# Slots made by VectorE alone, partly ahead or inside the first set, and attention's q and k loaded half a unit sooner

## Chip, cores and metric

One core of one Trainium2 chip runs the kernel. The metric is device time in microseconds (us). TensorE is PE, VectorE DVE, ScalarE ACT, GpSimd POOL; SP is the queue that issues the transfers.

## What is computed

```python
scores = matmul(q, k.T) / sqrt(64)                 # q, k, v: 4 x 8 heads x 576 x 64
attn = matmul(scores * gamma_h ** (i - j) * (i >= j), v)
x = attn as 2304 tokens x 512
x = relu(x @ w_in) ** 2 @ w_out                    # w_in 512 x 2048
p = domain_probs / (domain_probs.sum(-1) + 1e-9)
out = sum over e < 4 of p[:, e] * (relu(x @ w1[e]) @ w2[e])   # w1[e] 512 x 1024
```

All of it is float32. Wherever a product is large, each operand is a high part (rounded to fp32r) and a low part (the rest), and a product is three matmuls: high*high, high*low, low*high.

## The kernel before

**Attention** runs over 16 units (a batch and a pair of heads). A unit n has two steps, (n, 0) with three chunks of 128 tokens and (n, 1) with the other two. In step s PE adds to a running state (`update`), makes the scores of the next step (`scores`), which DVE masks out of PSUM (`masked`: L304 for three chunks, L306 for two), then does the masked scores times v (`inner`) and the state part (`outer`). `finish` splits the result into `xh` (ACT, L375) and `xl` (DVE, L377). After step (n, 0) `prepare(n + 2)` lets POOL scale k (L272) and q (L274); after (n, 1) `load(n + 3)` puts q, k, k in its other layout (`k_n`) and v into SP's queue. The tiles of unit n + 3 take the places of unit n, so each transfer waits until PE has read these.

From step (3, 0) on, `tick(2)` after each step takes two steps of the list `work`: the conversion of the first weights, which arrive as 64-bit floats. `from_f64` makes a piece of 256 columns in seven steps: one ACT step (L102), five DVE steps (L104 to L114), and one that issues an ACT copy and two POOL subtractions (L119 to L121). The last one is followed by `load_piece` (L81), which puts the load of a further piece into SP's queue; it takes the place of the piece just converted, so it waits for DVE's L114. The step list is worked off in the program's order, and each engine and SP's queue runs its own instructions in that order.

**First MoE**: eight chunks of 256 hidden units, five groups of tokens (four of 512, one of 256). `layer1` of a job (chunk, group) runs before `layer2` of the job before it; at the start two more `layer1` go ahead. `tick(pace[0])` follows each bank that is emptied.

**Second MoE**: 16 chunks, in two passes: groups 0, 1 and 4, then groups 2 and 3. A pair of groups goes through `layer1_pair`, in which seven products of half size (Strassen's scheme in Winograd's form) replace eight. It reads seven "slots", each a half-matrix in high and low part, kept where the tokens of the first MoE were (`xh_`, `xl_`). `slots` makes them out of `yacc`, the first MoE's result: `parts` casts a half on ACT (L579) and subtracts on DVE for one column block and on POOL for the other (L580), `minus` forms differences on DVE (L587). In the first change of stage (first MoE to second) slots 4 and 5 go after the last use of group 2, slot 6 after that of group 3. In the second (first pass to second) all slots are made after the last pair of the first pass. Before that, `scale` and `rescale` bring each group to a power of two (L546 to L569).

In `layer1_pair` a bank is accumulated into twice: the product A11 goes to b1, ACT copies it (L509), then A12 is added onto it; DVE adds L503 stand between the other products in the same way. `relu_split` ends it (ACT L478, DVE L479). In the first set of each pass `tick(steps)` between the products takes steps of `work`. `split_w1` and `split_w2` cast (ACT) and subtract (POOL, both L125) the weights of the second MoE; in the second pass `drain` issues all of `split_w2` of the next chunk before the next pair.

Of the kernel before, what the change touches and what calls it, by code (L numbers as in the profile page):

```python
# [6 lines left out]
F32 = mybir.dt.float32  # L7
# [7 lines left out]
B, H, S, D = 4, 8, 576, 64  # L15
NT, DM = 2304, 512
C = 128
# [16 lines left out]
def tile_kernel(ctx, tc, qT, kT, kn, vn, v4d, mask, qdec, kdec, wd, w, probs, out):  # L34
# [179 lines left out]
    def attention(a):  # L214
# [23 lines left out]
        def load(n):  # L238
            if n >= NU:
                return  # L240
            b, a = units[n]
            q_t = ap.tile([128, S], F32, name="q_t")
            k_t = kts[n % 3]
            k_n = ap.tile([C, 4, 2, D], F32, name="k_n")
            v_n = ap.tile([C, 4, 2, D], F32, name="v_n")

            dma = nc.scalar if n == 0 else nc.sync
            nc.sync.dma_start(out=q_t, in_=qT[b, a])
            dma.dma_start(out=k_t[:, :S], in_=kT[b, a])
            if n == 0:  # L250
                dma.dma_start(out=kd, in_=kdec)
            if n < NP:
                nc.sync.dma_start(out=mk[:, a], in_=mask[:, a])
            dma.dma_start(out=k_n, in_=kn[b, a].rearrange("p (c h d) -> p c h d", c=4, h=2))
            nc.sync.dma_start(out=v_n, in_=vn[b, a].rearrange("p (c h d) -> p c h d", c=4, h=2))
            if a == 0:
                dma.dma_start(out=v4[:, b * NP : (b + 1) * NP], in_=v4d[b].rearrange("p (a h d) -> p a h d", a=NP, h=2))
            if n < NP:
                nc.sync.dma_start(out=qd[:, a], in_=qdec[:, a])
            tl[n] = (q_t, k_t, k_n, v_n)  # L260

        qs = {}

        def prepare(n):

            if n >= NU:
                return
            b, a = units[n]
            q_t, _, k_n, _ = tl[n]
            k3 = k_n.rearrange("p c h d -> p (c h) d")  # L270
            t3 = kd[:, a].rearrange("p c h -> p (c h)").unsqueeze(2).to_broadcast([C, 8, D])
            (nc.vector if n == 0 else nc.gpsimd).tensor_tensor(out=k3, in0=k3, in1=t3, op=ALU.mult)  # L272
            qs[n] = ap.tile([128, S - C], F32, name="q_s")
            nc.gpsimd.tensor_tensor(out=qs[n], in0=q_t[:, C:], in1=qd[:, a, :], op=ALU.mult)  # L274
# [5 lines left out]

        def scores(s):
            n, h = s
            q_t, k_t, _, _ = tl[n]
            qk = pq.tile([C, 2, 512], F32, name="qk")
            for c in CS[h]:
                o, m = CH[c]
                w = o - CH[CS[h][0]][0]
                for j in range(2):
                    p = slice(64 * j, 64 * j + 64)
                    nc.tensor.matmul(  # L290
                        qk[:, j, w : w + m], k_t[p, o : o + C], q_t[p, o : o + m], start=True, stop=True,
                        skip_group_check=True,
                    )
            qks[s] = qk
# [14 lines left out]
        def update(n, c):  # L309

            if n >= NU:
                return
            _, _, k_n, v_n = tl[n]
            if c == 0:
                sts[n] = pst.tile([128, D], F32, name="state")
            st = sts[n]
            for j in range(2):
                nc.tensor.matmul(  # L318
                    st[64 * j : 64 * j + 64, :], k_n[:, c, j, :], v_n[:, c, j, :],
                    start=(c == 0), stop=(c == 3), skip_group_check=True,  # L320
                )
            sb = sbs[snap_n[0] % len(sbs)]
            snap_n[0] += 1
            for j in range(2):
                p = slice(64 * j, 64 * j + 64)
                nc.scalar.copy(out=sb[p, j, :], in_=st[p, :])
            snaps[n, c + 1] = sb
# [3 lines left out]
        def inner(s, c):  # L331

            n, h = s
            v_n = tl[n][3]
            o, m = CH[c]
            w = o - CH[CS[h][0]][0]
            if c == CS[h][0]:
                xos[s] = px.tile([128, 512], F32, name="xo")
            xo, pt = xos[s], pts[s]
            for j in range(2):  # L340
                vc = v_n[:, c, j, :] if c < 4 else v4[:, n, j, :]
                nc.tensor.matmul(  # L342
                    xo[64 * j : 64 * j + 64, w : w + m], vc, pt[:m, j, w : w + m],
                    start=(w == 0), stop=(c == 0), skip_group_check=True,
                )
# [39 lines left out]
            nc.vector.memset(t[:, S:], 0.0)  # L385
        for t in sbs:
            nc.gpsimd.memset(t, 0.0)
        load(1)
        load(2)
        prepare(0)  # L390
        scores(steps[0])
        masked(steps[0])
# [3 lines left out]
        for i, s in enumerate(steps):  # L396
            n, h = s
            nxt = steps[i + 1] if i + 1 < len(steps) else None
            un, uc = (n, 2) if h == 0 else (n + 1, 0)
            update(un, uc)  # L400
            if nxt:
                scores(nxt)
                masked(nxt)
            cs = CS[h]
            for c in cs[:-1]:
                inner(s, c)
            update(un, uc + 1)
            inner(s, cs[-1])
            for c in cs:
                if c:  # L410
                    outer(s, c)
            finish(s)
            if h == 0:
                prepare(n + 2)
            else:
                load(n + 3)
            if h == 0 and n in (1, 2, 3):
                load_piece()
            if s == (3, 0):
                queue_weights()  # L420
            tick(2)

    with tc.manual_schedule():
        with ExitStack() as a:
# [55 lines left out]
                out=lo, in0=h, scalar=0.0, in1=f32(hi), op0=ALU.max, op1=ALU.subtract  # L480
            )

        def layer1_pair(c, ga, gb, steps=0):


            w1h, w1l = w1s[c]
# [18 lines left out]
            u = [tp.tile([128, GT], F32, name="r") for _ in range(2)]  # L505
            u.append(cvp.tile([128, GT], F32, name="cv_tp"))
            b1 = bank()
            product(b1, A11, 0)
            nc.scalar.copy(out=u[0], in_=b1)  # L509
            b6 = bank()  # L510
            product(b6, S2, 3)
# [59 lines left out]
                op0=ALU.mult, op1=ALU.mult,  # L571
            )

        def parts(i, src, engines=(nc.vector, nc.gpsimd)):

            for k in range(2):
                yield
                hi = slot(xh_, i)[:, k, :]
                nc.scalar.copy(out=hi, in_=src[:, k, :])  # L579
                engines[k].tensor_tensor(  # L580
                    out=slot(xl_, i)[:, k, :], in0=src[:, k, :], in1=f32(hi), op=ALU.subtract
                )

# [2 lines left out]
                yield  # L586
                nc.vector.tensor_tensor(out=o[:, k, :], in0=x[:, k, :], in1=y[:, k, :], op=ALU.subtract)  # L587

        def slots(ga, gb):


            b11, b21 = yacc[ga][:, :2, :], yacc[ga][:, 2:, :]
            b12, b22 = yacc[gb][:, :2, :], yacc[gb][:, 2:, :]

            late = (nc.vector, nc.vector)

            def first():
                yield from parts(0, b11)
                yield from minus(b11, b12, b11)
                yield from parts(1, b11)  # L600
                yield from minus(b12, b22, b12)
                yield from minus(b11, b22, b11)
                yield from parts(3, b11)
                yield from parts(2, b12)

            def second():
                yield from parts(4, b21, late)
                yield from minus(b21, b21, b11)
                yield from parts(5, b21, late)

            return first(), second(), parts(6, b22, late)

        def layer2_1(c, g):
            w2h, w2l = w2s[c]
# [73 lines left out]
        mags.update({0: place(xh_, 1, 2), 1: place(xl_, 1, 2)})  # L688
        rest = place(xh_, 7, 7)[:2] + place(xl_, 7, 7)[:2]
        scaled = {NW1 + 4: 2, NW1 + 8: 3}  # L690
        sa, sb = slots(0, 1), slots(2, 3)
        pend = []
        for i, job in enumerate(jobs):
            c, gs = job
            g = scaled.get(c)
            drain(splits[split_w1, c])

            pace[0] = 3 if c in (p, q) else 4 if c == z else 2
            if job in ((NW1, (0, 1)), (NW1 + NW2, (2, 3))):
                drain((sa if c == NW1 else sb)[2])  # L700
            if g and gs == (0, 1):
                for k in range(KT):
                    magnitude(g, k, rest[k])
            if len(gs) > 1:
                if job == (NW1 + NW2, (2, 3)):
                    held.clear()
                    queue_weights()
                layer1_pair(c, *gs, steps=3 if job == (NW1 + NW2, (2, 3)) else 0)

                if job == (NW1, (0, 1)):  # L710
                    held.difference_update({(split_w2, NW1), (split_w1, NW1 + 1)})
# [1 line left out]
            elif job == (p, (4,)):  # L713
                s = layer1(c, *gs, lambda: scale(1, mags[1]))
                rescale(1, s)
                work.insert(0, sa[0])
            else:
                layer1(c, *gs)
            if i == last[c]:
# [1 line left out]
            if job == (p, (3,)):  # L721
                s = scale(0, mags[0])
            if job == (q, (2,)):
                work.insert(0, sa[1])
            if job == (q, (3,)):
                work.insert(0, sa[2])
            if job == (z, (0, 1)):
                drain(splits[split_w2, z])
                work[:0] = sb
            if g and gs == (4,):  # L730
                rescale(g, s)
            pend.append((i, job))

            while i > 1 and len(pend) > 1:
                j, done = pend.pop(0)
                drain(splits[split_w2, done[0]])
                layer2(done)
                if j == last[done[0]]:
                    queue_weights((split_w2, done[0] + 2))
                    if c >= NW1 + NW2:  # L740
                        drain(splits.get((split_w2, done[0] + 2)))
            if job == (p, (3,)):
                rescale(0, s)
# [67 lines left out]
```

## Time and profile before

| what | value |
|---|---|
| median of three runs | 1256.74 us (1250.98 to 1257.46) |
| the profiled execution | 1251.88 us, its span 1250.1 us |
| PE busy | 1223.1 us, 98% |
| DVE, POOL, ACT busy | 840.6 us, 526.2 us, 452.4 us |
| granted TensorE clock | full speed in every slice |

Busy times are sums over the whole span. A matmul of 512 columns counts as busy for 390 ns, though 48 of them in a row take 10.88 us, so PE's idle time is a little less than the time lost between matmuls.

### The profile page before, as it was taken

The page shows a single profiled execution, that of the slowest core. Times are in us where ns is not written, and L with a number is a line of the kernel's source. Part 1 is how long each engine was busy: PE and PEld are TensorE (multiplying, and loading weights), DVE is VectorE, ACT ScalarE, POOL GpSimd, SP SyncE. Part 2 cuts the span into 40 slices and gives each one's busy share as a digit, 9 for nine tenths or more (in the row PEclk, how much of TensorE's full clock was granted, in tenths as well). Part 3 has the DMA queues.
Part 4 walks back from the last instruction along what each step waited for, and adds up shares of the span by engine and source line. Part 5 has one row for each costly group of instructions (what it writes and reads, how often), then busy time and mean ns, then how long its engine had stood idle before and what let it go on. Part 6 is the DMA issues. An engine that isn't in the chain of part 4 may idle for free.

```text
span 1250.1 us, 17901 instructions
## 1 busy us (share of the span) xinstructions
PE 1223.1 (98%) x6576; PEld 1027.6 (82%) x6576; DVE 840.6 (67%) x1406; ACT 452.4 (36%) x1109; POOL 526.2 (42%) x635
## 2 busy tenths in 40 slices
PE   7989999999999998999999999999999999999998
PEld 6778888888888886888888888888778888888887
DVE  3775677787877687356756666565865676767665
ACT  3545433333333334533323323232335333333330
POOL 4555545555555445443422334222354343434340
PEclk9999999999999999999999999999999999999999
DMA  9741111111111000111111111110041111111111
GB/s 336 255 143 43 43 49 45 47 47 43 51 44 51 26 1 18 55 59 40 43 42 35 34 51 42 43 35 34 20 150 42 60 50 52 51 51 51 51 43 67
DMA packets 41303, 76.31 MB, mean 61 GB/s; under 512 B 4864, under 2 KB 5888, under 8 KB 41216
## 3 DMA queue, kind: packets, MB, share of 16 engines
q1 hardware_dynamic: 40704, 74.47, 17.5%
q8 instruction: 51, 0.84, 0.3%
q10 hardware_dynamic: 512, 0.70, 0.2%
q14 instruction: 36, 0.29, 0.1%
HBM read 70.44 MB, written 4.72 MB: 60 GB/s over the span
## 4 chain that ended last, share of the span: by engine, by line
PE 90%; DVE 5%; ACT 2%; DMA 1%; issue 1%; POOL 1%; ACTq 0%; POOLq 0%; DVEq 0%; SPq 0%
PE o L653 30%; PE h L496 24%; PE h L462 18%; PE o L621 14%; PE xo L342 1%; DVE xl L580 1%; PE qk L290 1%; DMA k_n<-kn 1%; PE xo L354 1%; DVE y L587 1%; PE state L318 1%; DVE y L553 1%; DVE r L467 1%; ACT xh L579 1%; DVE y L629 0%
## 5 line engine op out<-in xcount | busy, mean ns | idle before, releaser
L653 PE MATMUL o<-w2hi,ghi 128*128 128x512 f32 x576 | 224.8, 390 | 2.7 <-DVE oacc L661 2.7
L661 DVE SCALAR_TENSOR_TENSOR oacc<-o,pr,oacc 128x512 f32<-128x512 f32 x270 | 197.1, 745 | 42.5 <-PE o L653 41.9
L653 PE MATMUL o<-w2hi,glo 128*128 128x512 f32 x576 | 224.3, 389 | 0.0
L653 PE MATMUL o<-w2lo,ghi 128*128 128x512 f32 x576 | 224.1, 389 | 0.0
L125 POOL TENSOR_TENSOR w2lo<-wraw,w2hi 128x256 fp32r<-128x256 f32 x128 | 94.3, 764 | 206.3 <-ACT w2hi L124 206.3
L496 PE MATMUL h<-xh,w1hi 128*128 128x512 f32 x448 | 174.8, 390 | 4.9 <-ACT r L509 3.8
L496 PE MATMUL h<-xl,w1hi 128*128 128x512 f32 x448 | 174.4, 389 | 0.0
L496 PE MATMUL h<-xh,w1lo 128*128 128x512 f32 x448 | 174.3, 389 | 0.0
L125 POOL TENSOR_TENSOR glo<-r,ghi 128x512 fp32r<-128x512 f32 (+1 forms) x80 | 96.5, 1207 | 148.0 <-ACT ghi L124 147.1
L462 PE MATMUL h<-xh,w1hi 128*128 128x512 f32 (+1 forms) x448 | 154.1, 344 | 1.3 <-DVE xl L377 1.3
L462 PE MATMUL h<-xl,w1hi 128*128 128x512 f32 (+1 forms) x448 | 154.0, 344 | 0.0
L462 PE MATMUL h<-xh,w1lo 128*128 128x512 f32 (+1 forms) x448 | 153.9, 344 | 0.0
L125 POOL TENSOR_TENSOR w1lo<-wraw,w1hi 128x256 fp32r<-128x256 f32 x112 | 89.3, 797 | 131.9 <-ACT w1hi L124 131.9
L503 DVE TENSOR_TENSOR r<-h,r 128x512 f32<-128x512 f32 x96 | 66.4, 691 | 95.5 <-PE h L496 89.4
L653 PEld LDWEIGHTS o<-w2hi,ghi 128*128 128x128 f32 x576 | 108.2, 188 | 26.0 <-DVE oacc L661 4.0
L653 PEld LDWEIGHTS o<-w2lo,ghi 128*128 128x128 f32 x576 | 108.1, 188 | 22.6
L653 PEld LDWEIGHTS o<-w2hi,glo 128*128 128x128 f32 x576 | 108.2, 188 | 21.7
L621 PE MATMUL o<-glo,w2hi 128*128 128x512 f32 (+1 forms) x320 | 118.1, 369 | 1.6 <-POOL glo L125 1.6
L621 PE MATMUL o<-ghi,w2hi 128*128 128x512 f32 (+1 forms) x320 | 117.9, 369 | 0.3 <-ACT ghi L124 0.3
L621 PE MATMUL o<-ghi,w2lo 128*128 128x512 f32 (+1 forms) x320 | 117.7, 368 | 0.0
L467 DVE TENSOR_TENSOR r<-r 128x512 f32<-128x512 f32 (+1 forms) x80 | 63.8, 798 | 69.8 <-ACT r L466 69.6
L496 PEld LDWEIGHTS h<-xh,w1hi 128*128 128x128 f32 x448 | 84.1, 188 | 24.0 <-ACT r L509 4.6
(97 smaller groups left out, 2090.4 us busy)
## 6 DMA issues: line engine op xcount, KB each, us to landing
wraw<-w SPq DMA_DIRECT2D x128, 256.0 KB, 2.7
wraw<-wd SPq DMA_DIRECT2D x64, 256.0 KB, 2.7
q_t<-qT SPq DMA_DIRECT2D x16, 288.0 KB, 4.4
out<-oacc SPq DMA_DIRECT2D x18, 256.0 KB, 2.0
kt<-kT SPq DMA_DIRECT2D x15, 288.0 KB, 5.0
v_n<-vn SPq DMA_DIRECT2D x16, 256.0 KB, 4.7
k_n<-kn SPq DMA_DIRECT2D x15, 256.0 KB, 5.0
qd<-qdec SPq DMA_DIRECT2D x4, 224.0 KB, 5.2
```

The costliest lines, as they stand in the source:

```text
L125: nc.gpsimd.tensor_tensor(out=lo, in0=src, in1=f32(hi), op=ALU.subtract)
L290: nc.tensor.matmul(qk[:, j, w : w + m], k_t[p, o : o + C], q_t[p, o : o + m], start=True, stop=True, skip_group_check=True,)
L318: nc.tensor.matmul(st[64 * j : 64 * j + 64, :], k_n[:, c, j, :], v_n[:, c, j, :], start=(c == 0), stop=(c == 3), skip_group_check=True,)
L342: nc.tensor.matmul(xo[64 * j : 64 * j + 64, w : w + m], vc, pt[:m, j, w : w + m], start=(w == 0), stop=(c == 0), skip_group_check=True,)
L354: nc.tensor.matmul(xo[64 * j : 64 * j + 64, w : w + m], sb[:, j, :], qs[n][:, o - C : o - C + m], start=False, stop=True, skip_group_check ...
L462: nc.tensor.matmul(h, wk(a, f, k), x[:, k, :], start=(n == 0), stop=(n == 3 * KT - 1))
L467: nc.vector.tensor_tensor(out=r, in0=r, in1=r, op=ALU.mult)
L496: nc.tensor.matmul(o, a[:, i, k, :], slot(x, j)[:, k, :], start=(first and n == 0), stop=(n == 5), skip_group_check=True,)
L503: v.tensor_tensor(out=o, in0=x, in1=y, op=ALU.add)
L621: nc.tensor.matmul(o, a[:, f, 128 * m : 128 * m + 128], x[:, f, :], start=(n == 0), stop=(n == 3 * FT - 1))
L653: nc.tensor.matmul(o, a[:, f, 128 * m : 128 * m + 128], x[:, f, :], start=(n == 0), stop=(n == 3 * FT - 1))
L661: nc.vector.scalar_tensor_tensor(out=acc, in0=o, scalar=pr[:, tt, e : e + 1], in1=acc, op0=ALU.mult, op1=ALU.add)
```

## The change

Attention: `load(n + 3)` without v comes after step (n, 0), right behind `prepare(n + 2)`; v follows after step (n, 1), by a function of its own. `tick` takes one step after (n, 0) and two after (n, 1).

Start of the first MoE: four `layer1` go ahead of the first `layer2` (three before), and `work` takes four steps at a time in the first three jobs.

Slots: every subtraction is on DVE. `slots` has a fourth part, `ahead`, with the cast of A11 and four of the differences. In the first change of stage it runs where the first part ran, and slot 6 is made inside the first set, by its ticks. In the second, A11 goes to slot 7, which no pair reads in the first pass, and `ahead` is put at the end of `work` half a pass earlier; the pairs of the second pass read slot 7.

Second pass: the weights of chunk 25's second layer are no longer issued before chunk 25's pair.

```diff
@@ attention
-            dma.dma_start(out=k_n, ...)
-            nc.sync.dma_start(out=v_n, in_=vn[b, a]...)
+            dma.dma_start(out=k_n, ...)
+            if n == 0:
+                load_v(n)
...
+        def load_v(n):
+            if n < NU:
+                b, a = units[n]
+                vs[n] = ap.tile([C, 4, 2, D], F32, name="v_n")
+                nc.sync.dma_start(out=vs[n], in_=vn[b, a].rearrange("p (c h d) -> p c h d", c=4, h=2))
...
-        load(1)
-        load(2)
+        for n in (1, 2):
+            load(n)
+            load_v(n)
...
             if h == 0:
                 prepare(n + 2)
+                load(n + 3)
             else:
-                load(n + 3)
+                load_v(n + 3)
...
-            tick(2)
+            tick(1 + h)
@@ second MoE
-        def layer1_pair(c, ga, gb, steps=0):
+        def layer1_pair(c, ga, gb, steps=0, s0=0):
...
-            product(b1, A11, 0)
+            product(b1, A11, s0)
...
-                engines[k].tensor_tensor(
+                nc.vector.tensor_tensor(
                     out=slot(xl_, i)[:, k, :], in0=src[:, k, :], in1=f32(hi), op=ALU.subtract
                 )
...
-        def slots(ga, gb):
+        def slots(ga, gb, s0=0):
...
+            def ahead():
+                yield from parts(s0, b11)
+                yield from minus(b11, b12, b11)
+                yield from minus(b12, b22, b12)
 
             def first():
-                yield from parts(0, b11)
-                yield from minus(b11, b12, b11)
                 yield from parts(1, b11)
-                yield from minus(b12, b22, b12)
                 yield from minus(b11, b22, b11)
                 yield from parts(3, b11)
                 yield from parts(2, b12)
...
-            return first(), second(), parts(6, b22, late)
+            return ahead(), first(), second(), parts(6, b22)
@@ the jobs
-        sa, sb = slots(0, 1), slots(2, 3)
+        sa, sb = slots(0, 1), slots(2, 3, 7)
...
-            pace[0] = 3 if c in (p, q) else 4 if c == z else 2
-            if job in ((NW1, (0, 1)), (NW1 + NW2, (2, 3))):
-                drain((sa if c == NW1 else sb)[2])
+            pace[0] = 4 if i < 3 else 3 if c in (p, q) else 4 if c == z else 2
+            if job == (NW1, (0, 1)):
+                drain(sa[2])
+                work.insert(0, sa[3])
+            if job == (NW1 + NW2, (2, 3)):
+                drain(sb[3])
...
-                layer1_pair(c, *gs, steps=3 if job == (NW1 + NW2, (2, 3)) else 0)
+                steps = 3 if job == (NW1 + NW2, (2, 3)) else 2 if job == (NW1, (0, 1)) else 0
+                layer1_pair(c, *gs, steps, 7 if c >= NW1 + NW2 else 0)
...
-                work.insert(0, sa[0])
+                work[:0] = sa[:2]
...
             if job == (q, (2,)):
-                work.insert(0, sa[1])
-            if job == (q, (3,)):
                 work.insert(0, sa[2])
             if job == (z, (0, 1)):
                 drain(splits[split_w2, z])
-                work[:0] = sb
+                work[:0] = sb[1:]
             if g and gs == (4,):
                 rescale(g, s)
+                if g == 3:
+                    work.append(sb[0])
...
-            while i > 1 and len(pend) > 1:
+            while i > 2 and len(pend) > 1:
...
-                    if c >= NW1 + NW2:
+                    if c >= NW1 + NW2 and done[0] != z:
                         drain(splits.get((split_w2, done[0] + 2)))
```

## Rows read from the trace of the kernel before

**Rows 1.** Stretches: PE, weight loads, DVE, ACT, POOL busy (instructions); clock, DMA share, GB/s.
```profile
438.17:497.72 59.55, 54.31 (x283) 44.98 (x282) 49.81 (x71) 24.98 (x52) 30.76 (x28) 1.00 0.03 9
497.72:894.41 396.69, 396.69 (x1928) 335.88 (x1927) 245.34 (x389) 132.18 (x316) 140.96 (x189) 1.00 0.12 42
894.41:938.95 44.54, 39.77 (x183) 31.77 (x181) 32.72 (x52) 16.85 (x41) 19.77 (x24) 1.00 0.31 107
```

**Rows 2.** Chain of waits, whole span: start, us, what; two stretches of matmuls.
```profile
104.32 10.88 PE o L621 x48
126.08 2.87 PE h L462 x24
```

**Rows 3.** Chain of waits in attention.
```profile
14.13 0.99 PE qk L290 x12
...
46.95 0.87 PE qk L290 x12
...
51.29 0.87 PE qk L290 x12
...
54.77 5.20 DMA k_n<-kn
...
81.15 0.87 PE qk L290 x12
...
86.62 0.73 DVE cv_b L114
```

**Rows 4.** PE's waits from 14 to 88 us: total, times, longest.
```profile
PE xo L342 <- DVE pt L304: 3.5, 4, 1.3
PE h L462 <- DVE xl L377: 1.3, 1, 1.3
PE state L318 <- POOL k_n L272: 1.2, 1, 1.2
```

**Rows 5.** SP's queue in order of time.
```profile
53.40 0.33 SPq L81 DMA_DIRECT2D wraw<-wd  x1
53.83 0.37 SPq L248 DMA_DIRECT2D q_t<-qT  x1
```

**Rows 6.** SP's waits, 0 to 90 us: total, times, longest.
```profile
SPq L81 <- DVE cv_b L114: 33.1, 7, 8.3
...
SPq L248 <- PE qk L290: 5.2, 6, 1.6
```

**Rows 7.** DVE in order of time, in attention.
```profile
43.24 1.24 DVE L114 SCALAR_TENSOR_TENSOR cv_b<-wraw,cv_tp 128x256 f32<-128x256 uint32 x1
...
52.21 1.12 DVE L114 SCALAR_TENSOR_TENSOR cv_b<-wraw,cv_tp 128x256 f32<-128x256 uint32 x1
...
58.96 0.42 DVE L114 SCALAR_TENSOR_TENSOR cv_b<-wraw,cv_tp 128x256 f32<-128x256 uint32 x1
```

**Rows 8.** POOL in order of time, in attention.
```profile
43.02 1.18 POOL L274 TENSOR_TENSOR q_s<-q_t,qd 128x448 f32<-128x448 f32 x1
```

**Rows 9.** PE's waits from 438 to 498 us.
```profile
PE h L496 <- ACT r L509: 1.8, 1, 1.8
PE o L621 <- POOL glo L125: 1.6, 3, 0.7
PE h L496 <- DVE cv_tp L503: 1.2, 1, 1.2
```

**Rows 10.** Slot subtractions, 438 to 498 us: ns min/median/max, first and last start.
```profile
L580 DVE TENSOR_TENSOR xl<-y,xh x10: 674/748/1777, 454.5 to 490.9; 128x512 fp32r<-128x512 f32 x10
...
L580 POOL TENSOR_TENSOR xl<-y,xh x4: 1297/1345/1737, 455.0 to 466.2; 128x512 fp32r<-128x512 f32 x4
```

**Rows 11.** PE's waits from 880 to 940 us.
```profile
PE o L653 <- DVE oacc L661: 2.7, 3, 1.6
PE h L496 <- ACT r L509: 2.0, 1, 2.0
```

**Rows 12.** Chain of waits at the second change of stage.
```profile
929.20 2.86 DMA wraw<-w
```

More of the change, by code (lines that the diff above doesn't have):

```diff
@@ L244, in load @@
             k_n = ap.tile([C, 4, 2, D], F32, name="k_n")
-            v_n = ap.tile([C, 4, 2, D], F32, name="v_n")
             dma = nc.scalar if n == 0 else nc.sync
@@ L254, in load @@
             dma.dma_start(out=k_n, in_=kn[b, a].rearrange("p (c h d) -> p c h d", c=4, h=2))
-            nc.sync.dma_start(out=v_n, in_=vn[b, a].rearrange("p (c h d) -> p c h d", c=4, h=2))
+            if n == 0:
+                load_v(n)
             if a == 0:
@@ L259, in load @@
                 nc.sync.dma_start(out=qd[:, a], in_=qdec[:, a])
-            tl[n] = (q_t, k_t, k_n, v_n)
-        qs = {}
+            tl[n] = (q_t, k_t, k_n)
+        vs, qs = {}, {}
+        def load_v(n):
[3 more added lines that the diff above has]
+                nc.sync.dma_start(out=vs[n], in_=vn[b, a].rearrange("p (c h d) -> p c h d", c=4, h=2))
         def prepare(n):
@@ L268, in prepare @@
             b, a = units[n]
-            q_t, _, k_n, _ = tl[n]
+            q_t, _, k_n = tl[n]
             k3 = k_n.rearrange("p c h d -> p (c h) d")
@@ L282, in scores @@
             n, h = s
-            q_t, k_t, _, _ = tl[n]
+            q_t, k_t, _ = tl[n]
             qk = pq.tile([C, 2, 512], F32, name="qk")
@@ L312, in update @@
                 return
-            _, _, k_n, v_n = tl[n]
+            k_n, v_n = tl[n][2], vs[n]
             if c == 0:
@@ L333, in inner @@
             n, h = s
-            v_n = tl[n][3]
+            v_n = vs[n]
             o, m = CH[c]
@@ L572, in rescale, with parts @@
             )
-        def parts(i, src, engines=(nc.vector, nc.gpsimd)):
+        def parts(i, src):
             for k in range(2):
@@ L587, in minus @@
                 nc.vector.tensor_tensor(out=o[:, k, :], in0=x[:, k, :], in1=y[:, k, :], op=ALU.subtract)
-        def slots(ga, gb):
+        def slots(ga, gb, s0=0):
             b11, b21 = yacc[ga][:, :2, :], yacc[ga][:, 2:, :]
             b12, b22 = yacc[gb][:, :2, :], yacc[gb][:, 2:, :]
-            late = (nc.vector, nc.vector)
+            def ahead():
+                yield from parts(s0, b11)
+                yield from minus(b11, b12, b11)
+                yield from minus(b12, b22, b12)
             def first():
-                yield from parts(0, b11)
-                yield from minus(b11, b12, b11)
                 yield from parts(1, b11)
-                yield from minus(b12, b22, b12)
                 yield from minus(b11, b22, b11)
@@ L606, in second @@
             def second():
-                yield from parts(4, b21, late)
+                yield from parts(4, b21)
                 yield from minus(b21, b21, b11)
-                yield from parts(5, b21, late)
-            return first(), second(), parts(6, b22, late)
+                yield from parts(5, b21)
+            return ahead(), first(), second(), parts(6, b22)
         def layer2_1(c, g):
```

## Prediction

> **What bounds the kernel.** I read the busy table first: PE is busy 98% of the span at the full clock (2.4 GHz throughout), so a change that removes no matmul can win back only PE's gaps. In the busy time by stretch the long stretch of the first pass shows PE busy for all of its 396.69 us, and so does the first MoE until its last jobs; the gaps lie in three places, two of them in [rows 1]. I size each by its count of matmuls: 48 of 512 columns take 10.88 us, 0.227 each, and 24 of 256 take 2.87, 0.120 each [rows 2].
>
> - Attention. Unit 8 begins at 46.95 and unit 9 at 51.29: an undisturbed unit takes 4.34 us. From 14.13 to 81.15 there are 14 units, 67.0 us, where 14 x 4.34 = 60.8: 6.3 lost [rows 3]. A further 1.3 is waited at the end [rows 4].
> - First change of stage, 59.55 us long [rows 1]. By the program it holds 170 matmuls of 512 columns, 96 of 256 and 16 of one column (about 0.1): 38.6 + 11.5 + 1.6 = 51.7. Lost: 7.8.
> - Second change of stage, 44.54 us [rows 1]: 156 and 24 matmuls, 35.4 + 2.9 = 38.3. Lost: 6.3.
>
> Together 21.7 us, the most that the change could give.
>
> **Attention, part by part.** PE's waits show three causes: 3.5 us in four waits for the masking L304, 1.2 for the scaled `k_n`, 1.3 at the end for `xl` [rows 4]; what the count has beyond these (6.3 - 3.5 - 1.2 = 1.6) is waits too short for that view.
>
> *The `k_n` wait.* SP issued a weight piece (L81) at 53.40 and q of unit 11 only at 53.83 [rows 5]; the `k_n` behind it landed at 54.77 + 5.20 = 59.97 [rows 3], and POOL and PE waited. The piece had waited for DVE's L114, 1.12 us long at 52.21 [rows 7]. These holds sum to 33.1 us, the longest 8.3 [rows 6]. Counting the steps (seven a piece, three a unit from unit 3), pieces are now issued after steps (5, 1), (7, 1), (10, 0), (12, 1) and (14, 1). The only one that follows a step (n, 0) now stands behind that load's q and k instead of before it; the others stand behind v, and their L114 runs at the latest early in the next unit, while SP's next q waits for PE's scores in its middle. So no piece holds up a load, and I take the 1.2 as gained (bounds 0 and 1.3).
>
> *The L304 waits.* Between `finish(n, 0)` and the large masking DVE had two conversion steps, now one. Some steps last far longer than others: L114 0.42 us at 58.96 but 1.12 and 1.24 at 52.21 and 43.24 [rows 7], the last while POOL makes q_s (43.02, for 1.18) [rows 8]. At 52.21 the slot held one DVE step: it ended 2.04 us after unit 9's start, and no wait over 0.15 us followed [rows 3, 4, 7]. So about 2.1 us after the unit's start is the limit, and one step at its worst length so far (1.24, from 0.92 after the start: 2.16) costs 0.1. By the count of steps 9 of the 13 slots hold a DVE step, so 0.9 stays, and I leave 0.3 for ACT's part. Of 5.1 (3.5 + 1.6) 3.9 is gained. Bounds: 5.1 if no step meets POOL; at the other end each step waits out a whole q_s and then takes its own 0.42: 0.92 + 1.18 + 0.42 = 2.52 after the start, 0.45 late, nine times 4.0.
>
> *The end.* L114 stood before the last `xl` for 0.73 us [rows 3]; the slot after (15, 0) now holds ACT's step. I take 0.4 (bounds 0 and 0.7).
>
> Attention: 1.2 + 3.9 + 0.4 = 5.5 gained.
>
> *What is put off.* 26 steps of two become 13 units of three: 13 of 52 conversion steps move behind attention, and 17 of chunk 0's second layer are open. The first three jobs take 3 x 2 x 4 = 24 steps, and that layer is needed only after four `layer1` of 24 matmuls, 21.8 us. Even one piece after the other, a piece in the worst 2 us of its DVE rows [rows 7] plus its ACT and POOL parts, 2.5 pieces fit. I cost this at nothing; without that cover it would be at most some 5 us.
>
> **First change of stage, 7.8 lost.** PE waits 1.6 for POOL's glo, 1.8 for ACT's copy L509, 1.2 for the add L503 [rows 9]; the rest is shorter waits, and some 1.0 for `scale`, which is left alone.
>
> Four subtractions move from POOL to DVE here. On POOL one takes 1.35 us, on DVE 0.67 at best, but up to 1.78 where both engines work at once [rows 10]. DVE thus does four more at 0.67, 2.7 us, and is spared about as much blocking: three others stretched by up to 1.1 each. The count of DVE's time to the last slot of `first` comes out within some 0.3; what follows starts some 1.5 us sooner, since the pair of blocked instructions at its end goes. That removes the shorter wait at `layer2` of the small group, 1.4. POOL's own queue, eight weight splits ahead of glo, shifts by as much as PE, so of the 1.6 I take 0.45. Slot 6 (two casts, two subtractions) no longer stands before L509 and L503: L509 comes about 2 us sooner, but PE arrives 1.9 sooner too, so 0.45; L503's 1.2 goes, but the two subtractions now stand before the add that the last product needs, and of it 0.9 comes back: 0.4 with the short waits there. Sum 1.4 + 0.45 + 0.45 + 0.4 = 2.7. Bounds: 6.8 gained, all except `scale`; or 1.3 lost, if the four subtractions at 1.78 each put some 4 us more on DVE.
>
> The Trainium skill's page "SBUF — State Buffer", section "Who interferes with whom", says that a DVE instruction with two SBUF inputs and a POOL instruction that reads SBUF cannot run together, and the later one waits for the whole of the earlier; 1.78 against 0.67, a difference near POOL's duration, agrees. [...]
>
> **Second change, 6.3 lost.** PE waits 2.7 for DVE's accumulation L661, whose banks DVE empties late because the slots stand before it; by the count of matmuls 3.7. DVE had 18 slot instructions there, now 16, and POOL four, now none; one of DVE's waited 1.2 for POOL in turn. 16 x 0.62 and the L661 between put the eighth L661 some 3 us sooner; 0.6 of 3.7 stays, 3.1 gained (bounds 1.5 and 3.7). PE waits 2.0 (2.3 by the count) for L509 [rows 11]: ACT was to cast weights that landed only after a transfer begun at 929.20, 2.86 long [rows 12]. Those four casts now come in the next `layer2`. Its 16 ticks then hold exactly the casts (5 steps) and the next first layer (11), so the transfer before the pair of chunk 26 starts late as well, by my count about 1 us after that pair instead of 2: 0.65 comes back there. Gained 1.7 (bounds 0 and 2.3). Sum 4.8. `ahead` runs in the first pass, where DVE is busy 245.3 of 396.7 us [rows 1]: nothing.
>
> **Sum.** 5.5 + 2.7 + 4.8 = 13.0 us. The profiled execution took 1251.88, 1.8 more than its span; that gives 1238.9. The other runs lie at 1250.98, 1256.74 and 1257.46; the median, 1256.74, is 4.9 above the profiled one. From the mean of the four, 1254.3, the forecast is 1241.3, and I predict 1241.
>
> **Rivals.**
> 1. *The early load does nothing.* SP waits for PE's scores before q [rows 6] in either order, so only the held piece matters, and `k_n` could stay late by another one: the 1.2 is not gained. 1242.5. Against it: the order above.
> 2. *POOL keeps blocking the one step.* Nine slots at 0.45 leave 4.0 instead of 0.9: gain 9.9, 1244.4. For it: two of three L114 shown are blocked [rows 7, 8].
> 3. *DVE is the limit at both changes of stage.* Seven subtractions at 0.6 come on top and no blocking goes: 4.2 less, gain 8.8, 1245.5. For it: DVE is busy 49.8 of 59.6 us at the first [rows 1]. Against: 1.78 [rows 10].
> 4. *Both 2 and 3, and the late cast moves whole to chunk 26:* gain 13.0 - 3.1 - 4.2 - 1.7 = 4.0, 1250.3: no change that can be told.
> 5. *Slower: the pieces hold the loads.* Each of five pieces stands before q and k of some unit. A `k_n` has about 3.5 us to spare (two units to its use, less its landing at 5.20 and POOL). Five holds like the longest, 8.3 [rows 6], cost 5 x 4.8 = 24: 11 more than the gain, 1265. It decides from a hold of 3.5 + 13/5 = 6.1. Against: each L114 has run by then.
>
> **Chances.** Forecast 0.5, rivals in order 0.1, 0.13, 0.12, 0.1, 0.05. Less than about 0.5% (6.3 us) cannot be told from no change here. Faster is the forecast and rivals 1 to 3: 0.85; same 0.10; slower 0.05. Range 1233 to 1250: below, the gain near its bound (18 from 1251); above, rival 4. The forecast's own is 1236 to 1246.
>
> **What would show it.** Right: units of 4.34 us nearly all through, L304 waits under 1.5, no `k_n` wait, the first MoE beginning near 82; no POOL L580, short L580 on DVE; the first set still waiting for L509, the second pass's wait at chunk 25 gone and a small one at 26. Wrong: L304 late with one step, waits inside the first set over 3 us, or a gap at the first `layer2`.

## Result and profile after

The changed kernel takes 1239.65 us (median of 4 runs, 1238.53 to 1240.66); the kernel before took 1254.37 on the same chip (4 runs, 1250.98 to 1257.46). The ratio is 0.9887, 95% interval 0.9868 to 0.9906. The profiled execution took 1239.68 with a span of 1237.9: 12.2 us less than before, where the sum of the prediction was 13.0. In the changed file the lines have moved: the scores are L296, the masking L310, the state copy L332, `xl` L383; a set's adds are L512 and its copy L518; glo is awaited by `layer2` L630, the accumulation is L670, a slot's subtraction L589.

First the changed kernel's stretches of the two changes of stage, in the columns of [rows 1], between the same events.

```profile
433.62:490.51 56.89, 53.97 (x283) 44.93 (x282) 48.61 (x75) 25.14 (x52) 25.21 (x24) 1.00 0.03 10
...
887.20:926.50 39.30, 39.22 (x184) 32.36 (x183) 29.08 (x49) 14.30 (x34) 15.09 (x18) 1.00 0.31 108
```

The first is 2.66 us shorter than in [rows 1], the second 5.24. DVE's column is the one to read: in the first it does 75 instructions in 48.61 us, where it did 71 in 49.81. It has four more subtractions and is busy 1.2 us less.

PE's waits in the changed kernel, from 13 to 90, 425 to 500 and 870 to 950 us, in the columns of [rows 4].

```profile
PE h L471 <- DVE xl L383: 0.8, 1, 0.8
PE xo L348 <- DVE pt L310: 0.2, 1, 0.2
...
PE o L630 <- POOL glo L125: 1.0, 2, 0.7
PE h L505 <- ACT r L518: 0.7, 1, 0.7
PE h L505 <- DVE cv_tp L512: 0.7, 1, 0.7
PE po L569 <- DVE r L557: 0.3, 1, 0.3
...
PE h L505 <- ACT r L518: 0.3, 1, 0.3
```

Attention: L310 falls from 3.5 to 0.2, the `k_n` wait is gone and the last one falls from 1.3 to 0.8 [rows 4]. First change of stage: glo 1.6 to 1.0 (one of its three waits, 0.56, was the small group's), the copy 1.8 to 0.7, the add 1.2 to 0.7, the last at another product than before [rows 9]. Second: the accumulation's 2.7 is gone and the copy's 2.0 is 0.3 [rows 11].

What is left in attention is seen in the chain of waits of the changed kernel, in one slot, and in POOL's row at that time.

```profile
41.15 0.49 ACT xh L381
41.66 0.56 DVE xl L383
42.22 1.05 DVE cv_tp L104
43.27 0.88 DVE pt L310
44.19 0.66 PE xo L348 x8
```

```profile
41.98 1.14 POOL L280 TENSOR_TENSOR q_s<-q_t,qd 128x448 f32<-128x448 f32 x1
```

The one conversion step that is left (L104, which takes 0.28 us at best) ends at 43.27, 0.15 after POOL's q_s, and the masking, the `xo` product and the rest follow it. By the matmuls' starts the masking is late in four units, by 0.1 to 0.25 us.

### The profile page after: what moved, and what is told of

The parts are those of the page before. It is cut to its first block, busy times and chain, and to the rows that moved or that the text cites. A ratio compares the mean times of both kernels' runs of the same rounds, so it can differ in the third digit from the quotient of the medians.

```text
span 1237.9 us, 17902 instructions
## 1 busy us (share of the span) xinstructions
PE 1221.7 (99%) x6576; PEld 1027.7 (83%) x6576; DVE 843.7 (68%) x1414; ACT 451.0 (36%) x1109; POOL 517.9 (42%) x627
## 4 chain that ended last, share of the span: by engine, by line
PE 92%; DVE 4%; ACT 2%; DMA 1%; issue 1%; POOL 0%; ACTq 0%; DVEq 0%
PE o L662 30%; PE h L505 24%; PE h L471 18%; PE o L630 15%; PE xo L348 2%; PE qk L296 1%; DVE xl L589 1%; PE xo L360 1%; PE state L324 1%; DVE y L596 1%; DMA k_n<-kn 0%; DVE r L476 0%; DVE y L638 0%; DVE y L562 0%; ACT xh L588 0%
## 5 line engine op out<-in xcount | busy, mean ns | idle before, releaser
L670 DVE SCALAR_TENSOR_TENSOR oacc<-o,pr,oacc 128x512 f32<-128x512 f32 x270 | 196.9, 745 | 41.2 <-PE o L662 40.7
L512 DVE TENSOR_TENSOR r<-h,r 128x512 f32<-128x512 f32 x96 | 66.4, 691 | 86.7 <-PE h L505 77.4
L630 PE MATMUL o<-glo,w2hi 128*128 128x512 f32 (+1 forms) x320 | 118.1, 369 | 1.0 <-POOL glo L125 1.0
L630 PE MATMUL o<-ghi,w2hi 128*128 128x512 f32 (+1 forms) x320 | 117.8, 368 | 0.0
L630 PE MATMUL o<-ghi,w2lo 128*128 128x512 f32 (+1 forms) x320 | 117.7, 368 | 0.0
```

Of the source, the lines that this page charges most:

```text
L512: v.tensor_tensor(out=o, in0=x, in1=y, op=ALU.add)
L630: nc.tensor.matmul(o, a[:, f, 128 * m : 128 * m + 128], x[:, f, :], start=(n == 0), stop=(n == 3 * FT - 1))
L670: nc.vector.scalar_tensor_tensor(out=acc, in0=o, scalar=pr[:, tt, e : e + 1], in1=acc, op0=ALU.mult, op1=ALU.add)
```

## Experiments

A time without a range is a single execution. Places are compared in the profiled executions. A matmul's lateness is the distance to the next matmul's start less the 0.227 or 0.120 us of [rows 2].

In attention I compare from the scores of unit 2 to the second scores of unit 15. Unit 1 starts with its score matmuls 0.21 us apart in some executions and 0.11 in others, of the same kernel, which moves all of attention by up to 1 us. Undisturbed that distance is 13 x 4.34 + 2.28 = 58.7.

**The two halves alone.** One kernel has the attention of after and the slots of before, the other the reverse.

> The attention part alone (q and k loaded sooner, three conversion steps a unit, four first-layer jobs ahead), slots as before. Theory (three places that add up): the first MoE begins 4.5 us sooner, as in the changed kernel, and the two changes of stage lose what they lost before (7.8 and 6.3): about 4.5 us faster than before. Rival (what attention wins is given back, because the 13 conversion steps that were put off and the fourth early job crowd the first MoE): a gap of some us at the first second-layer job or at chunk 1, and under 2 us gained in the span.

> The slot part alone (subtractions on VectorE, slot 6 in the first set, the part ahead, chunk 25's casts later), attention and the first jobs as before. Theory: attention ends near 87.5 us as before, the first change of stage loses 5.1 instead of 7.8 and the second 1.3 instead of 6.3: 7.7 us faster. Rival (part of this gain came only because attention ended sooner): less than 6 us.

Attention alone: 1248.04 (ratio 0.9943, 0.9926 to 0.996). Unit 2 to 15 takes 59.8 where before took 64.8 and after 60.2. The first change of stage takes 59.55 us (432.38 to 491.93), exactly as before, and the waits are those of before, here from 870 to 950 us:

```profile
PE o L662 <- DVE oacc L670: 2.7, 3, 1.6
PE h L505 <- ACT r L518: 2.1, 1, 2.1
```

Slots alone: 1245.89 (0.9921, 0.9899 to 0.9943). Its first change of stage takes 56.87 us (441.19 to 498.06), where after takes 56.89. Its attention waits at the same places as before (from 13 to 92 us):

```profile
PE xo L342 <- DVE pt L304: 4.1, 4, 1.5
PE h L462 <- DVE xl L377: 1.3, 1, 1.3
PE state L318 <- POOL k_n L272: 1.1, 1, 1.1
```

Unit 2 to 15 takes 66.8 in this execution, 1.9 more than in before, part of it a stretch at half clock (last section); two executions of the same attention differed by that much here. The halves touch different places, and at the first change of stage neither disturbs the other. In the medians they gain 7.8 and 9.9 us, where 4.5 and 7.7 were expected: together more than the 14.7 of the whole. But the kernel before has a median of 1255.79 beside the halves and of 1254.37 beside the whole, and its executions range from 1250.98 to 1258.27, so this sum decides nothing.

**The halves of the attention change.** First the early load with two steps in every slot, then one step after (n, 0) with the load where it was.

```diff
@@ early load, two steps
-            tick(1 + h)
+            tick(2)
@@ late load, fewer steps
             if h == 0:
                 prepare(n + 2)
-                load(n + 3)
             else:
+                load(n + 3)
                 load_v(n + 3)
```

> The changed kernel, but two conversion steps after every step of attention again; the loads stay early. Theory (steps and loads cure different waits): the masking waits of 3.5 us come back, the wait for the scaled k stays away because the weight piece now stands behind q and k in the queue; 14 units take 65.5 us instead of 62.3. Rival (the early load does nothing by itself): the wait of 1.2 us for the scaled k comes back as well, 14 units take 67 us as before.

> The changed kernel, but q, k and v of unit n + 3 all loaded after step (n, 1) as before; one and two conversion steps stay. Theory: SP waits for TensorE's reads in either order, and with this count of steps no weight piece that has to wait stands in front of q and k (the only one after a step (n, 0) follows VectorE's step of the unit before): 14 units take 62.3 us as in the changed kernel, so the early load is worth nothing once the steps are fewer. Rival (the early load is what keeps k in time): a wait for the scaled k of 1 us or more, 14 units take 63.5 us or more.

Early load with two steps: 1243.80; unit 2 to 15 takes 63.6, 1.2 less than before. The `k_n` wait is gone and the masking's is nearly whole (13 to 92 us):

```profile
PE xo L348 <- DVE pt L310: 3.0, 4, 0.9
PE h L471 <- DVE xl L383: 1.3, 1, 1.3
PE state L324 <- ACT st L332: 0.2, 1, 0.2
```

Late load with fewer steps: 1239.99; unit 2 to 15 takes 60.0, as in after, and there is no `k_n` wait either:

```profile
PE h L471 <- DVE xl L383: 0.8, 1, 0.8
PE xo L348 <- DVE pt L310: 0.2, 1, 0.2
```

So each half removes the `k_n` wait by itself, and only the fewer steps remove the rest. With them the early load is worth nothing that shows (at most some 0.3). SP's queue shows how each half does it. In before the piece ahead of the late `k_n` was held for 4.8 us, from behind this transfer until 53.40 [rows 5], with q, k and `k_n` behind it:

```profile
48.23 0.33 SPq L255 DMA_DIRECT2D v_n<-vn  x1
```

With the early load and two steps these three are issued ahead of that piece, as the prediction has it (`k_n` at 51.72, the piece at 54.33). With the late load and fewer steps the piece still stands ahead of them, but is held for 2.3 us only (issued at 50.23).

**Where the step stands.** None after (n, 0), three after (n, 1): no conversion step is left ahead of the large masking.

```diff
-            tick(1 + h)
+            tick(3 * h)
```

> The changed kernel, but all three conversion steps of a unit come after step (n, 1) and none after (n, 0). Theory (what is left in attention is the one step that stands before the large masking while GpSimd scales q; before the small masking there is about 1 us to spare, and a step takes 0.3 to 0.4 where nothing blocks it): 14 units take 61.0 to 61.3 us instead of 61.8 to 62.7. Rival (three steps in a row make the small masking late): 62.5 us or more, with waits for the small masking.

1241.27; unit 2 to 15 takes 60.8, 0.6 more than after, where about 1 us less was expected. The masking L310 is never late, so the cause was right, but another wait came, seen in its waits from 13 to 90 us and in its chain from 39.84 on:

```profile
PE state L324 <- ACT st L332: 1.3, 2, 0.7
PE h L471 <- DVE xl L383: 0.8, 1, 0.8
PE xo L348 <- DVE pt L312: 0.2, 1, 0.2
```

```profile
39.84 0.34 DVE cv_b L114
...
40.20 0.02 ACT cv_tp L102
...
40.55 0.20 ACT st L332
...
40.76 0.22 ACT st L332
...
41.02 0.34 PE state L324 x4
```

With three steps in a row one slot can hold a piece's last DVE step (L114) and the next piece's first ACT step (L102). ACT then waits in L102 for DVE, and the state copies L332 that PE needs stand behind it. It happens at 40 and at 71 us, 0.9 and 0.8 late by the matmuls' starts. The end of attention, outside the distance compared, takes 0.4 longer than in after as well: there the small masking L312 is late, as the rival had it, though by far less.

**POOL's subtractions back** for slots 0 to 3, one column block each, with all else as in after (slots 4 to 6 were on DVE alone in the kernel before too):

```diff
-                nc.vector.tensor_tensor(
+                (nc.gpsimd if k and i < 4 else nc.vector).tensor_tensor(
```

> The changed kernel, but the subtractions of the second column block of slots 0, 1, 2 and 3 are on GpSimd again (four at the first change of stage, three at the second); all else is as changed. Theory (GpSimd's subtractions cost VectorE in blocking as much as they spare it, and the blocked pair at the end of the first part is what the small group's second layer waited for): the first change of stage loses 6.3 us instead of 5.1, with the wait at the small group back at 1.2 to 1.4; the second loses 2 to 2.5 instead of 1.3. Rival (VectorE is simply the limit there): with seven subtractions of 0.6 us taken off it the two places lose less than in the changed kernel, 3 us in all instead of 6.4.

1240.76. Waits from 425 to 500 (the first two rows of it) and 870 to 950 us:

```profile
PE o L630 <- POOL glo L125: 1.6, 3, 0.7
PE h L505 <- ACT r L518: 0.8, 1, 0.8
...
PE o L662 <- DVE oacc L670: 0.7, 1, 0.7
```

The gaps of the small group's second layer are back, 1.3 us (0.48 at 461.95 and 0.83 at 462.55), as in before (0.51 and 0.82). PE's waits name glo, but POOL's queue is not the cause: in before POOL has ended its two subtractions 0.80 us ahead of glo and waits for ACT's cast of `ghi`, and this cast waits for DVE's square L467, held to 1.51 us beside them (0.41 in after). DVE's row, then two of POOL's:

```profile
466.73 1.51 DVE L467 TENSOR_TENSOR r<-r 128x256 f32<-128x256 f32 x1
...
464.96 2.99 POOL L580 TENSOR_TENSOR xl<-y,xh 128x512 fp32r<-128x512 f32 x2
468.75 0.86 POOL L125 TENSOR_TENSOR glo<-r,ghi 128x256 fp32r<-128x256 f32 x1 [0.80 <-ACT ghi L124]
```

With POOL's subtractions back the rows repeat: the square takes 1.50, and glo starts 0.80 after POOL's pair. So it is the blocked pair on DVE, as expected. The stretch of the first change takes 58.05 us, 1.16 more than in after, and DVE is busy longer with four instructions fewer (columns of [rows 1]):

```profile
432.00:490.05 58.05, 54.22 (x283) 45.00 (x282) 49.27 (x71) 25.13 (x52) 30.84 (x28) 1.00 0.03 10
```

In the second change the accumulation is late by 0.83 instead of 0.24: 0.6, less than expected. The total hides both, as this execution's attention ended 1.6 us sooner.

**Slot 6 ahead of the first set**, as the kernel before had it:

```diff
-                drain(sa[2])
-                work.insert(0, sa[3])
+                drain(sa[3])
...
-                steps = 3 if job == (NW1 + NW2, (2, 3)) else 2 if job == (NW1, (0, 1)) else 0
+                steps = 3 if job == (NW1 + NW2, (2, 3)) else 0
...
+            if job == (q, (3,)):
+                work.insert(0, sa[3])
```

> The changed kernel, but slot 6 is made before the first set of the second MoE again, by VectorE, as before. Theory: the two casts and two subtractions stand before the copy and the adds again: the wait for the copy grows from 0.9 to 1.8 us, the wait for the second add (about 1.2) is back, and the 0.9 before the last product goes: the set loses 3.2 us instead of 2.1. Rival (it makes no difference where they stand, they only move the wait within the set): 2.1 us in the set, within 0.3.

1240.45. The copy is 1.95 late again (0.91 in after) and the 0.9 before the last product is gone; the add's wait does not come back. The copy's row, 425 to 500 us:

```profile
PE h L505 <- ACT r L518: 1.8, 1, 1.8
```

From 484.6 to 488 PE ran at a granted clock of 0.55, so it reached the add later; what the add would have cost at full clock is not seen. Slot 6 inside the set thus wins the copy's 1.0 and puts a wait of 0.9 at the last product; what it wins in all is not shown.

**Fewer weight splits ahead of glo**: around the small group and in group 2's first layer a tick takes one step of `work` instead of three, and three again after it.

```diff
+            if job == (q, (2,)):
+                pace[0] = 1
...
+            if job in ((q, (4,)), (q, (2,))):
+                pace[0] = 1 if job == (q, (4,)) else 3
```

> The changed kernel, but the first weights of the second MoE are worked off more slowly while the small group's second layer of chunk 6 and the first layer of group 2 of chunk 7 are issued (one step of the list at a time instead of three), so that three of the eight weight splits stand in GpSimd's queue before that group's low part instead of eight. Theory (the 1.6 us wait at that group's second layer is GpSimd's queue): the wait falls to 0.3 or less, and the first change of stage loses 4 us instead of 5.1. Rival (the low part is late because the square is late on VectorE): the wait stays over 1 us.

1238.40. Its waits from 425 to 500 us:

```profile
PE h L505 <- ACT r L518: 1.5, 1, 1.5
PE po L569 <- DVE r L557: 0.4, 1, 0.4
PE h L505 <- DVE cv_tp L512: 0.3, 1, 0.3
```

Glo's 1.3 at group 2's second layer is gone, so the splits ahead of it were the cause. But PE now comes sooner to the first set, and the copy's lateness grows from 0.91 to 1.67; the last product's falls from 0.90 to 0.43. Net 1.0 by these places; the stretch (433.34 to 488.90) is 1.3 shorter, as the matmul behind each longer wait is some 0.1 late too.

**The early issue of chunk 25's weights put back**, a single execution first and then more of them:

```diff
-                    if c >= NW1 + NW2 and done[0] != z:
+                    if c >= NW1 + NW2:
```

> The changed kernel, but the weights of chunk 25's second layer are issued before its pair again. Theory: the wait of 2 us for the copy of the first product comes back at chunk 25's pair and the one of 0.5 us at chunk 26's pair goes; the second change of stage loses 2.9 instead of 1.3, or a little less where the transfer starts sooner now. Rival (the transfer begins sooner because the slots are done sooner, so the wait would have gone by itself): no wait over 0.7 us at chunk 25's pair.

> The changed kernel with chunk 25's second-layer weights issued before its pair again, now timed, to see in how many executions the wait of 2 us is followed by a drop of the granted clock. Theory (the wait brings the drop on): a mean granted clock under 1.000 in most executions, and 1241 to 1243.5 us: 1.6 of wait and up to 1.8 of half clock over the changed kernel. Rival (the drop in the one profile was chance): 1.000 in most executions and 1241.2 us.

1243.42, then 1242.67 (1242.11 to 1243.71) against 1239.80 for after on the same chip. The copy waits again, 2.2 us and 2.6 us late at chunk 25, and nothing at chunk 26. What follows the wait costs as well. The first of the two kernels in three stretches, columns as in [rows 1], the clock third from the end:

```profile
920.00:923.00 3.00, 1.24 (x6) 0.70 (x4) 0.00 (x0) 0.96 (x3) 2.55 (x5) 1.00 0.91 275
924.20:927.50 3.30, 3.30 (x9) 2.58 (x8) 1.24 (x2) 0.60 (x1) 0.00 (x0) 0.51 0.32 112
927.80:930.00 2.20, 2.20 (x11) 1.81 (x10) 1.37 (x3) 0.63 (x1) 0.00 (x0) 1.00 0.00 0
```

PE is idle for more than half of the first, and in the second its clock is 0.51 of full speed, the lower of its two levels (1.2 GHz): 9 matmuls in 3.3 us, where the third has 11 in 2.2.

**All together**: fewer splits ahead of glo, `tick(3 * h)`, POOL for slot 6's subtractions, and no early issue of any next chunk's weights in the second pass; beside it after itself on the same chip.

```diff
-            tick(1 + h)
+            tick(3 * h)
...
-            return ahead(), first(), second(), parts(6, b22)
+            return ahead(), first(), second(), parts(6, b22, e6)
...
-        sa, sb = slots(0, 1), slots(2, 3, 7)
+        sa, sb = slots(0, 1, 0, nc.gpsimd), slots(2, 3, 7)
...
-                    if c >= NW1 + NW2 and done[0] != z:
-                        drain(splits.get((split_w2, done[0] + 2)))
```

> The changed kernel with four edits together: all three conversion steps after step (n, 1); fewer weight splits ahead of the low part of group 2; slot 6's subtractions on GpSimd within the first set, where it has nothing else to do; and no early issue of second-layer weights before any pair of the second pass. Theory (each takes one remaining wait: 1 us in attention, 1.6 at group 2's second layer of which 0.8 comes back at the copy of the first product, 0.4 to 0.9 before the last product of the set, 0.6 at chunk 26): 2.5 to 3.5 us less than the changed kernel on the same chip, about 1237. Rival (the waits move to the next place that VectorE's backlog reaches, the copy of the first product above all): within 1 us of the changed kernel.

> The changed kernel once more, beside the version with four edits and the kernel before on one chip. Theory (the kernel before has waits of about 2 us after which the granted clock of TensorE drops for some microseconds in part of its executions; the changed kernel has none that long): a mean granted clock of 1.000 in nearly all executions of the changed kernel and 0.996 to 0.998 in most of the kernel before, which puts the measured gain some 2 us over the 12.2 us that the two profiles show. Rival (the clock has nothing to do with the waits): the same share of executions under 1.000 in both.

1238.85 (1238.71 to 1238.98; ratio to before 0.9878, 0.9861 to 0.9895) against 1239.80 (1238.53 to 1241.27; 0.9884, 0.9865 to 0.9902). The ranges overlap: no difference that can be told, where 2.5 to 3.5 us were expected; the rival's bound of 1 us held. Its waits at the late places are two, 425 to 500 us, and none from 870 to 950:

```profile
PE h L505 <- ACT r L518: 1.5, 1, 1.5
PE po L569 <- DVE r L557: 0.3, 1, 0.3
```

Glo, the last product and chunk 26 are mended, and the copy takes back half: the first change of stage takes 55.04 us (435.19 to 490.24), 1.85 less than in after. But `tick(3 * h)`, which was expected to gain 1 us, costs 1.1 to 1.5 from unit 2 to the first MoE (65.1, where the two profiled executions of after take 64.0 and 63.6). Without that edit it should come out some 1 us lower; that was not run.

## Why the prediction came out

**Attention.** Forecast 5.5 gained, measured 5.1 from unit 2 on: 4.6 in the units (64.8 to 60.2) and 0.5 at the end (1.3 to 0.8; forecast 0.4). The first MoE begins 4.5 us sooner, at 83.16 for 87.67, because unit 2 began 0.6 later in this execution. 1.5 us are still lost in the units, where the forecast left 1.2. By the matmuls' starts the masking has 0.7 of it (forecast 0.9) and ACT's state copies 0.55 (0.30 and 0.25 in two units; forecast 0.3). The size was right, its division was not: the 1.2 of the `k_n` wait was put down to the early load, and the fewer steps alone remove it too. So the first rival is right that beside the fewer steps the early load does nothing, yet not in its price, since nothing was lost by it.

The Trainium skill's page "SBUF — State Buffer", section "Who interferes with whom", names `tensor_scalar` among the operations that can take the port pair that DVE shares with POOL. The row of L104 at 42.22, 1.05 for 0.28 beside POOL's q_s, agrees; the prediction had used the rule for two SBUF inputs alone.

**What was put off.** No wait stands at the first jobs of the MoE after `xl`'s, so the cover was there.

**First change of stage.** 2.7 forecast, 2.66 measured, out of terms that missed by about the same in both directions; that the sum came out so close is luck:

| term | forecast | measured (lateness before, after) |
|---|---|---|
| small group's second layer | 1.4 | 1.2 (1.33, 0.14) |
| glo at group 2 | 0.45 | 0 (1.32, 1.32) |
| the copy in the first set | 0.45 | 1.0 (1.91, 0.91) |
| adds in the first set | 0.4 | 0.4 (1.31, 0.90) |

The first term came by the mechanism that was forecast, the blocked pair on DVE. The second was sized on the 1.6 of [rows 9], of which 0.56 was the small group's. At group 2 POOL's splits stand ahead of glo as before and moved with PE. That delay at glo gives ACT's copy time, and the copy's term came out larger for it. The run with fewer splits shows the exchange: 1.3 gone at glo, 0.8 more at the copy. The two terms were in large part one: how early PE reaches the set. The add's return by 0.9 at the last product came as forecast.

**Second change.** 4.8 forecast. The stretch is 5.24 shorter, and 0.5 comes back at chunk 26, outside it: 4.7. The accumulation is late by 0.24 where it was late by 3.2 (0.45, 1.81 and 0.97); the casts of chunk 25 had 2.19 and have nothing, chunk 26 has 0.5 (forecast 0.65). Of the accumulation's 3.0, the largest term, 0.6 comes back with POOL's subtractions; the rest is put down to the slot parts made in the first pass, as the forecast counted, but no run took these back alone, so it is not shown. Issuing the casts later is worth 1.7 by the places, and with them put back the median is 2.9 us higher, half clock after the wait included.

**DVE as the limit**, the third rival, fell by the run with POOL's subtractions back: with four instructions fewer DVE is busy 49.27 us instead of 48.61. They cost DVE more than they spare it. **Pieces holding the loads**, the fifth: the forecast's "no piece holds up a load" was too strong, but the rival's condition was far from met. SP's waits in the changed kernel, 0 to 90 us, and rows of its queue:

```profile
SPq L81 <- DVE cv_b L114: 21.4, 4, 10.2
...
47.01 0.33 SPq L268 DMA_DIRECT2D v_n<-vn  x1
49.71 0.33 SPq L81 DMA_DIRECT2D wraw<-wd  x1
...
69.75 10.95 SPq L81 DMA_DIRECT2D wraw<-wd  x2
```

The longest hold, 10.2 us, and the one after it, 8.7, come when the last load of attention has been issued: nothing of attention stands behind them. One hold of size has loads behind it, 2.3 us up to 49.71. That is under the 6.1 named and under the 4.8 after which `k_n` was late in before, and no wait for `k_n` followed.

**The base.** 13.0 from the mean of four times gave 1241.3; the median came out at 1239.65 although the span gave 0.8 less than forecast. The gain in the medians (14.7) is larger than in the spans (12.2), and the mean clock goes with that: below 1.000 in most executions of the kernel before, though not in its profiled one, and in hardly any of the changed kernel (last section). The forecast had no term for this.

## What to carry to other kernels

Where two engines hold each other up, as DVE and POOL did here, giving the whole job to one of them can take less of that engine's own time than sharing it: compare its busy time by stretch, and not only the other engine's. The engine that a wait names may itself have been waiting: follow the chain from PE's late operand back to the row that ran too long. Terms that lie one after the other on PE's way are not separate: size the place where PE arrives sooner together with the next one that makes it wait. A step that is taken out from ahead of one engine's urgent work must be followed into the queues of the others that it visits, as the three steps in a row showed on ACT.

## What the runs showed of the hardware

Waits of about 2 us in the middle of dense work were followed, within some microseconds, by a stretch at half clock, in every profiled kernel that kept the wait at chunk 25 except the one of before. After 2.2 us of lateness the granted clock was 0.51 from 924.20 to 927.50 in the kernel above; in the same kernel's second profile, after 2.6 us, it was 0.50 from 924.40 to 927.00; in the kernel with slot 6 ahead of the first set it was 0.55 after 1.95 us at that set's copy; in the kernel with attention alone, 0.54 after 2.28 us at 925.15. The last one's stretch, columns as in [rows 1]:

```profile
928.00:931.50 3.50, 3.50 (x10) 2.77 (x9) 1.71 (x3) 0.60 (x1) 0.31 (x1) 0.54 0.44 137
```

In the kernel with slots alone a stretch of it followed a wait of 1.52 us for the masking at 81.07, in the same columns:

```profile
83.00:85.00 2.00, 2.00 (x21) 1.76 (x18) 0.92 (x4) 0.84 (x4) 0.00 (x0) 0.55 0.00 0
```

So a wait can cost more than its length. Not every such wait has it: the profiled execution of before waited as long at chunk 25 (2.19) and stayed at 1.00, and the copy in the first set was late by 1.91 there and by 1.93 with attention alone, at full clock after it. The mean granted clock of an execution goes with its time where it is lowest. Of 18 executions of the kernel before that list it, 5 have a mean clock of 1.000 and take 1251.88 to 1253.78; the 6 at 0.996 and 0.997 take 1255.35 to 1258.27; the 7 between take 1252.02 to 1254.65, which is hardly more than at 1.000. Of the changed kernel's nine, eight are at 1.000 and one at 0.999. With chunk 25's weights issued early it is 0.998 or 0.999 in all five. Which executions get the drop was not settled; when the wait starts was not varied.
